# A hand-ordered opening of attention and MoE, put in another order on all five engines

## The chip, the core and the metric

The kernel runs on one core of a Trainium2 chip. The metric is the device time of one execution in microseconds (us). The kernel before was timed three times: 304.38, 303.49 and 304.17, median 304.17.

## What is computed

The reference chains two parts. Sliding-window causal attention over 8 batches of 8 heads with 576 tokens and 64 channels, in which a query sees itself and the 63 keys ahead of it, gives 4608 tokens of 512 channels; a feed-forward layer with the gate `h * cos(h)` follows.

```python
scores = scale * np.matmul(q, k.transpose(0, 1, 3, 2))
mask = (rel >= 0) & (rel < window)           # rel = query - key, window 64
scores = np.where(mask, scores, -1000000000.0)
attn = np.exp(scores - np.max(scores, axis=-1, keepdims=True))
attn = attn / (np.sum(attn, axis=-1, keepdims=True) + 1e-09)
x = np.matmul(attn, v)                       # then tokens x (heads * channels)
h = x @ w_in                                 # 512 -> 2048
g = h * np.cos(h)
out = g @ w_out                              # 2048 -> 512
```

## The kernel before

The feed-forward part goes over nine tiles of 512 tokens. In eight of them it runs in a steady state: TensorE (PE) is fed with `h` products (L468) and `out` products (L707 or L555) while the attention of the next batch is laid between them by planned times (`at`, `pump`). The first 58 us are different. There the first tile has nothing to hide behind, and every step is put out by hand: the string `FIRST` (L46) lists 303 tokens, and the loop at L671 carries them out one after the other. Each token issues a few instructions on one or two engines. So the place of a token in the string is the place of its instructions in the queue of their engine; the five engines take their queues strictly in order and meet only at semaphores. A last letter gives the engine: d is VectorE (DVE), a is ScalarE (ACT), p is GpSimd (POOL), s is a DMA from SyncE's queue (SP).

Work is cut by pairs of heads, p = 0 to 3, and a batch has 9 blocks of 64 queries. A group is four blocks of one pair; batch 0 has groups (p, 0) and (p, 1) for each pair. The tokens that matter, with their lines:

- `Lq0.p`, `Lk0.p`: q and k of one pair of batch 0 (`load_heads`, L155, a DMA from POOL's queue that casts to bf16; pair 0 comes as float32 by SP, `load_plain`, L162, and is cast by `cq` and `ck`). `Lq1`, `Lk1` are those of batch 1, `Lv0.c` a 128-token chunk of v, `Lwi.i` and `Lwo.i` quarters of w_in and w_out (L197, L200). `Lq2.c` and `Lk2.c` are 96-token chunks of batch 2 (L172).
- `io`, `mk`, `mc`: the distances by POOL (L137), the masks by DVE (L141 to L145), their bf16 copies by ACT (L149).
- `tq.p`, `tk.p`: 18 transposes of q or k on PE (L210); `pq`, `pk` copy them out of PSUM (L232, L234, L125). `Tq`, `Tk`, `Pq`, `Pk` are the same for batch 1.
- `s.p.g`: mask and scores of a group on PE (L314, L321); `m` its row maxima on DVE (L331); `e` four exponentials on ACT (L348); `i` the reciprocal of the sums on DVE (L358); `n` the normalising product, 128x512, on POOL or DVE (L365); `w` four transposes on PE (L381); `c` their copy (L389, carried out at L125).
- `zA`, `zB`, `zC`: each 64-token block of v must stand on both halves of the partitions; `spread_v` (L186) copies half a chunk to its neighbour, on DVE, POOL or by DMA on SP (L193).
- `v.a.g`: the values of two pairs on PE (L418); `x.a.g` copies them to `xT` (L425). `h.g.f` needs `x.0.g` and `x.1.g`: eight products with w_in (L432), half a token tile for two blocks of 128 features; `S.g.f` is the sine on ACT (L438), `g.g.f` the gate on DVE (L444). `o.q.m` is a quarter of an output tile on PE (L451).
- `Gs`, `Gm`, `Ge`, `Gi`, `Gn`, `Gw`, `Gc`, `Gp`: the same steps as s, m, e, i, n, w, c for the groups 8 to 18 (the rest of batch 0, and batch 1). Their maxima go by one instruction per block (L336).
- `f`: one 128x512 product that nobody reads (`keep_busy`, L129); eight of them run before the list.

Buffers join the queues. Transposes and values share three PSUM tiles (`ps_t`, L97), scores and `h` share five banks (L117, the last number of `s`, `Gs` and `h`), and a new user waits until the former one is read out. A DMA that POOL issues waits, as the eighth after another, for the landing of that one (its semaphore lane). After the list, `turn_k` (L248, planned at L610) transposes k of batch 2 by DMA on SP, chunk after chunk in the order 0 to 5, for the first scores of batch 2 (L299).

Of the kernel before, what the change touches and what calls it, by code (L numbers as in the profile page):

```python
# [10 lines left out]
def _safe_warn(msg, *a, **kw):  # L11
# [32 lines left out]


FIRST = (  # L46
# [19 lines left out]
)  # L66


# [1 line left out]
def kernel(  # L70
# [10 lines left out]
    B, H, S, D = q.shape  # L81
# [70 lines left out]
    def rows_tile(name):  # L152
        return ld.tile([128, NC * H * D], BF16, tag=name, name=name)

    def load_heads(name, b, p0=0, n=PAIRS):  # L155
        if (name, b) not in st:
            st[name, b] = rows_tile(name)[:, 0:PAIRS * RC * D].rearrange("p (a x) -> p a x", a=PAIRS)
        src = {"q": q, "k": k}[name][b, 2 * p0:2 * p0 + 2 * n]
        nc.gpsimd.dma_start(out=st[name, b][:, p0:p0 + n],
                            in_=src.rearrange("(a h) (p c) d -> (h p) a (c d)", h=2, c=RC))  # L160

    def load_plain(name):  # L162
        rows = moe.tile([128, 2, d_model], F32, tag="out", name="rows", bufs=OUTS).rearrange("p a f -> p (a f)")[:, 0:RC * D]
        st["rows", name] = rows
        nc.sync.dma_start(out=rows, in_={"q": q, "k": k}[name][0, 0:2].rearrange("h (p c) d -> (h p) (c d)", c=RC))
# [99 lines left out]
    for b in range(2, B):  # L265
        alone = NU // 2 if b == 3 else NU - 1
        steps = [(0, 2), (2, 4)], [(alone,)] + [(5, 7), (7, 9)] if b == 3 else [(4, 6), (6, 8), (alone,)]
# [362 lines left out]
    for n in range(16):  # L630
        i, f = divmod(n, 4)
# [14 lines left out]
    def spread_first(lo, hi):  # L646
        return lambda i, engine: spread_v(0, i, engine, lo, hi)

    steps = {"f": keep_busy, "Lq0": lambda p: load_heads("q", 0, p, 1) if p else load_plain("q"),
             "Lk0": lambda p: load_heads("k", 0, p, 1) if p else load_plain("k"),  # L650
             "cq": lambda engine: cast_plain("q", engine), "ck": lambda engine: cast_plain("k", engine),
             "Lq1": lambda p: load_heads("q", 1, p, 1), "Lk1": lambda p: load_heads("k", 1, p, 1),
# [24 lines left out]
    for mt in range(1, n_mt):  # L677
# [5 lines left out]
        for ff in range(n_ff):  # L683
# [8 lines left out]
            e = ff % 2  # L692
# [54 lines left out]
```

## Time and profile before

| what | value |
|---|---|
| median of three runs | 304.17 us (303.49 to 304.38) |
| the profiled execution | 303.55 us |
| its span, first to last instruction | 301.8 us |
| PE busy | 291.2 us, 97% of the span |
| DVE, ACT, POOL busy | 234.7, 232.3, 209.2 us |
| granted PE clock, mean | 0.993 |
| first `h` product (L432) starts | 22.18 us |
| first `h` product of the second token tile (L468) starts | 57.45 us |

The profiled execution is 1.75 us longer than its span (what lies before the first and after the last instruction) and 0.62 us shorter than the median. PE is busy almost all the time from 14 us on, so the table is read by stages of the opening: when the `h` products can start, and where PE waits between there and 57 us. A row of the timeline has the start and length in us, the engine, the line, the operation, what is written from what, its count, and in brackets the idle time just before and what ended it.

### The profile page before, as it was taken

To read this page: it belongs to the slowest core of one execution; us is meant where nothing else is said; L and a number is where in the kernel's file an instruction comes from. 1 tells how busy PE (TensorE), PEld (TensorE's weight loads), DVE (VectorE), ACT (ScalarE), POOL (GpSimd) and SP (SyncE) were. 2 spreads that over 40 slices of the span, in tenths; PEclk is the share of its full clock that TensorE was granted. 3 is DMA by queue.
4 is the path that set the end of the run, shared out by engine and by line. 5 is a ranking of instruction groups with operands and counts; after the bars stand their busy time and mean duration, and the time that the engine had idled before them with its cause. 6 is when DMAs were issued, how large, how long until landed. Compare 5 with 4: busy or idle time off the path is not lost.

```text
span 301.8 us, 8513 instructions
## 1 busy us (share of the span) xinstructions
PE 291.2 (97%) x2916; PEld 164.0 (54%) x2947; DVE 234.7 (78%) x916; ACT 232.3 (77%) x781; POOL 209.2 (69%) x238
## 2 busy tenths in 40 slices
PE   8799999999999999999999999999999999999996
PEld 3677854644455445444454445444544454785485
DVE  4798788888887886788668875887588658985794
ACT  5988699877987699869986999699978997304610
POOL 8979568986999589987998799878995860000000
PEclk9989999999999999999999999999999999999999
DMA  7999999999999994999999997999599935003013
GB/s 148 180 208 164 198 193 142 104 127 147 232 160 102 229 139 87 102 143 235 149 102 139 209 177 96 144 209 165 103 108 134 203 65 168 0 3 141 1 37 104
DMA packets 158732, 41.47 MB, mean 137 GB/s; under 512 B 146976, under 2 KB 154336, under 8 KB 158688
## 3 DMA queue, kind: packets, MB, share of 16 engines
q0 software_dynamic: 100192, 18.06, 79.8%
q1 hardware_dynamic: 58352, 22.79, 41.9%
q8 instruction: 23, 0.38, 0.5%
q14 instruction: 21, 0.17, 0.2%
q10 hardware_dynamic: 144, 0.07, 0.1%
HBM read 36.70 MB, written 9.44 MB: 153 GB/s over the span
## 4 chain that ended last, share of the span: by engine, by line
PE 88%; DMA 4%; DVE 3%; issue 2%; ACT 1%; POOL 1%; POOLq 0%; DVEq 0%
PE h_ps L468 37%; PE out_ps L707 27%; PE out_ps L555 8%; PE out_ps L451 4%; PE h_ps L432 3%; PE s_ps L299 3%; PE o_ps L400 3%; DMA w_in<-in_moe_w_in_dram 2%; DMA k<-in_k_dram 2%; PE tq_ps L213 1%; PE s_ps L321 1%; ACT e L348 1%; PE tk_ps L210 1%; DVE s L336 1%; PE tw_ps L381 1%
## 5 line engine op out<-in xcount | busy, mean ns | idle before, releaser
L468 PE MATMUL h_ps<-xT,w_in 128*128 128x512 bf16 x497 | 114.3, 379 | 1.0
L696 DVE TENSOR_TENSOR gT<-h_ps,sin 128x512 bf16<-128x512 f32 x128 | 85.2, 688 | 25.8 <-ACT sin L693 25.2
L693 ACT ACTIVATE sin<-h_ps 128x512 f32<-128x512 f32 x128 | 73.8, 598 | 37.1 <-PE h_ps L468 35.2
L348 ACT ACTIVATE e<-s,negm 128x128 f32<-128x128 f32 (+1 forms) x256 | 97.1, 382 | 1.7 <-POOL v L125 1.0
L707 PE MATMUL out_ps<-w_out,gT 128*128 128x512 bf16 x372 | 82.9, 379 | 1.7 <-issue 1.6
L365 POOL TENSOR_TENSOR w<-e,rden 128x512 bf16<-128x512 f32 (+1 forms) x68 | 69.1, 1032 | 18.0 <-DVE rden L358 15.1
L468 PEld LDWEIGHTS <-w_in 128*128 128x128 bf16 x512 | 49.0, 98 | 54.5
L707 PEld LDWEIGHTS <-gT 128*128 128x128 bf16 x384 | 36.5, 98 | 43.1
L336 DVE CUSTOM_DVE_ANT_0 s<-s_ps,mask 128x128 f32<-128x128 f32 (+1 forms) x256 | 56.0, 277 | 1.7 <-PE s_ps L321 1.4
L348 ACT ACTIVATION_READ_ACCUMULATOR e<-s,negm 128x1 f32 x256 | 48.1, 188 | 0.0
L176 POOL DMA_DIRECT2D q<-in_q_dram x36 | 28.6, 796 | 10.7 <-DMA q<-in_q_dram 5.4
L182 POOL DMA_DIRECT2D v<-in_v_dram x40 | 34.2, 870 | 1.2 <-DMA q<-in_q_dram 1.1
L176 POOL DMA_DIRECT2D k<-in_k_dram x36 | 28.6, 795 | 2.7 <-DMA v<-in_v_dram 1.9
L358 DVE RECIPROCAL rden<-den 128x4 f32<-128x4 f32 (+1 forms) x73 | 12.2, 167 | 18.3 <-ACT e L348 17.9
L125 POOL COPY v<-v 64x1536 bf16<-64x1536 bf16 (+3 forms) x16 | 22.9, 1433 | 0.4
L336 DVE DVE_READ_ACCUMULATOR2_ANT negm<- 128x1 f32 x256 | 21.2, 83 | 0.0
L125 DVE CAST xT<-o_ps 128x512 bf16<-128x512 f32 x24 | 15.5, 679 | 4.7 <-PE o_ps L400 4.5
L432 PE MATMUL h_ps<-xT,w_in 128*128 128x256 bf16 x128 | 14.8, 273 | 0.4 <-DMA w_in<-in_moe_w_in_dram 0.4
L451 PE MATMUL out_ps<-w_out,gT 128*128 128x512 bf16 x60 | 14.3, 380 | 0.3 <-issue 0.2
L432 PEld LDWEIGHTS <-w_in 128*128 128x128 bf16 x128 | 12.2, 98 | 2.1 <-DMA w_in<-in_moe_w_in_dram 0.7
L555 PEld LDWEIGHTS <-sums 128*128 128x128 bf16 x136 | 12.2, 98 | 1.9 <-DVE sums L500 0.4
L348 ACT ACTIVATE e<-s_ps,negm 128x128 f32<-128x128 f32 x32 | 11.3, 383 | 1.2 <-DVE negm L331 1.0
(88 smaller groups left out, 309.7 us busy)
## 6 DMA issues: line engine op xcount, KB each, us to landing
out_dram<-out_sb SPq DMA_DIRECT2D x16, 512.0 KB, 7.7
v<-in_v_dram POOLq DMA_DIRECT2D x32, 128.0 KB, 5.9
q<-in_q_dram POOLq DMA_DIRECT2D x36, 96.0 KB, 8.5
k<-in_k_dram POOLq DMA_DIRECT2D x36, 96.0 KB, 8.8
w_in<-in_moe_w_in_dram POOLq DMA_DIRECT2D x4, 512.0 KB, 8.8
w_out<-in_moe_w_out_dram POOLq DMA_DIRECT2D x4, 512.0 KB, 11.4
q<-in_q_dram POOLq DMA_DIRECT2D x7, 144.0 KB, 6.1
k<-in_k_dram POOLq DMA_DIRECT2D x7, 144.0 KB, 5.8
```

The source lines that it names most:

```text
L125: {"a": nc.scalar.copy, "p": nc.gpsimd.tensor_copy}.get(engine, nc.vector.tensor_copy)(out, in_)
L176: nc.gpsimd.dma_start(out=st[name, b][:, c].rearrange("p (h d) -> p h d", h=H), in_=src.rearrange("h p d -> p h d"))
L182: nc.gpsimd.dma_start(out=vt.rearrange("p (h d) -> p h d", h=H), in_=v[b, :, c * 128:c * 128 + n, :].rearrange("h p d -> p h d"))
L336: nc.vector.tensor_tensor_reduce(out=s[:, u, c], in0=s_ps[:, u, c], in1=mask[:, 2 - j % 2 if j else 0, c], scale=-scale if b else -1.0, sc ...
L348: nc.scalar.activation(e[:, u, c], s[:, u, c], AF.Exp, bias=negm[:, u:u + 1], scale=1.0 if n < n_first else -1.0, accum_out=den[:, u:u + 1])
L365: (nc.gpsimd if engine == "p" else nc.vector).tensor_tensor(out=w[:, 0:u], in0=e[:, 0:u], op=ALU.mult, in1=rden[:, 0:u].unsqueeze(2).to_br ...
L432: nc.tensor.matmul(out=h_ps[:, half * e:half * e + half], lhsT=w_in_sb[:, ks, ff * 128:ff * 128 + 128], rhs=st["xT", 0][:, ks, half * g:ha ...
L468: nc.tensor.matmul(out=st["h", ff], lhsT=w_in_sb[:, ks, ff * 128:ff * 128 + 128], rhs=st["xT", mt][:, ks], start=start, stop=stop)
L555: nc.tensor.matmul(out=to[n_] if split else to[:, e], lhsT=lhs[name][f // 2][:, f % 2, 128 * e:128 * e + 128], rhs=rhs[name][:, f, lo:hi], ...
L693: nc.scalar.activation(sin, h_ps, AF.Sin, bias=math.pi / 2.0)
L696: nc.vector.tensor_tensor(out=gt[:, e], in0=h_ps, in1=sin, op=ALU.mult)
L707: nc.tensor.matmul(out=o_ps[e], lhsT=gT[ff // 2][:, ff % 2, ms * 128:ms * 128 + 128], rhs=w_out_sb[:, ff], start=ff == 0, stop=ff == n_ff - 1)
```

## The change

`FIRST` is replaced by a list with the same steps in another order. Some steps change their engine or their bank as well. The dictionary of steps gets six names for `keep_busy` in place of one. Nothing else differs.

```diff
-    "io Lq0.0 Lk0.0 mk cq.d mc ck.a tq.0 f.1 Lq0.1 pq.0.d Lk0.1 tk.0 f.1 pk.0.a s.0.0.0 Lq0.2 tq.1 f.1 tk.1 m.0.0 "
+    "Lk0.0 Lq0.0 Lq0.1 Lk0.1 io mk Lq0.2 cq.d tq.0 ck.d Lk0.2 Lq0.3 mc tk.0 pk.0.a pq.0.d s.0.0.0 tq.1 s.0.1.3 "
...
-    steps = {"f": keep_busy, "Lq0": lambda p: load_heads("q", 0, p, 1) if p else load_plain("q"),
+    steps = {"fa": keep_busy, "fb": keep_busy, "fc": keep_busy, "fd": keep_busy, "fe": keep_busy, "ff": keep_busy, "Lq0": lambda p: load_heads("q", 0, p, 1) if p else load_plain("q"),
```

What moves, token by token, where the prediction speaks of it:

- `io` stands behind two of POOL's loads instead of ahead of all; `ck` goes from ACT to DVE.
- `Lk0.3` stands behind `Lq1.0` and `Lq1.1`. `pk.2` goes from DVE to ACT and stands behind `e.0.1`; `s.3.0` stands ahead of `Tk.0`, and `Tk.1` behind `s.3.1`.
- `Lwi.0` stands ahead of `Lv0.0`, `Lwi.1` ahead of `Lv0.2`; `n.0.0`, `n.2.0` and `n.1.0` stand between these loads, `n.3.0` behind `Lwi.2`. `Lwi.3` stands ahead of `n.0.1` and `n.2.1`; `n.1.1` and `n.3.1` go to DVE.
- `zA.0` goes from DVE to POOL, `zB.0` and `zC` from SP's DMA to DVE, `zB.1` from SP's DMA to POOL.
- two of the three `f` move from the first 7 us to just before `Tk.1` and just before `v.0.0`; `w.0.1` and `w.2.1` stand behind the first `h`.
- `Lk2.5` stands far ahead, `Lk2.3` ahead of batch 1's normalisations, and `Lk2.0` and `Lk2.1` are the last loads of the list.

POOL's queue from the last k of the first loads to the last quarter of w_in. v0 is batch 0's v; a row `w<-e,rden` is one normalisation. Before:

```order
L159 DMA k_326<-in_k_dram 128x576
L182 DMA v0_77<-in_v_dram 128x8x64 x4
L198 DMA w_in_79<-in_moe_w_in_dram 128x4x512 x3
L365 TENSOR_TENSOR w_499<-e_398,rden_462 128x512
L365 TENSOR_TENSOR w_531<-e_297,rden_396 128x512
L365 TENSOR_TENSOR w_534<-e_453,rden_469 128x512
L365 TENSOR_TENSOR w_570<-e_473,rden_536 128x512
L365 TENSOR_TENSOR w_587<-e_389,rden_572 128x512
L365 TENSOR_TENSOR w_678<-e_538,rden_589 128x512
L365 TENSOR_TENSOR w_720<-e_579,rden_656 128x512
L198 DMA w_in_79<-in_moe_w_in_dram 128x4x512
```

And the same stretch of the change, in which w_492 is `n.2.0`, w_515 `n.1.0` and w_582 `n.3.0`:

```order
L198 DMA w_in_79<-in_moe_w_in_dram 128x4x512
L182 DMA v0_77<-in_v_dram 128x8x64 x3
L198 DMA w_in_79<-in_moe_w_in_dram 128x4x512
L365 TENSOR_TENSOR w_435<-e_230,rden_259 128x512
L182 DMA v0_77<-in_v_dram 128x8x64
L365 TENSOR_TENSOR w_492<-e_461,rden_481 128x512
L365 TENSOR_TENSOR w_515<-e_428,rden_484 128x512
L198 DMA w_in_79<-in_moe_w_in_dram 128x4x512
L365 TENSOR_TENSOR w_582<-e_486,rden_538 128x512
L125 COPY v0_77<-v0_77 64x512
L159 DMA q_261<-in_q_dram 128x576
L198 DMA w_in_79<-in_moe_w_in_dram 128x4x512
```

The quarters of w_in have moved between v and the normalisations, and a copy of v stands behind `n.3.0`.

DVE's queue ahead of the copy to xT that the first `h` needs; the rows `kT` and `qT` are Pk and Pq, `negm` maxima, `wT` the copies c. Before, from `Pq.1`:

```order
L125 COPY qT1_76<-tq_ps_434 128x576
L331 TENSOR_REDUCE negm_520<-s_ps_501 128x4
L358 RECIPROCAL rden_536<-den_474 128x4
L125 COPY v0_77<-v0_77 64x512
L125 COPY wT_555<-tw_ps_544 128x512
L358 RECIPROCAL rden_572<-den_390 128x4
L125 COPY wT_574<-tw_ps_550 128x512
L125 COPY v0_77<-v0_77 64x512
L125 COPY wT_577<-tw_ps_565 128x512
L358 RECIPROCAL rden_589<-den_539 128x4
L125 COPY wT_617<-tw_ps_591 128x512
```

And of the change, from `i.3.0` to `x.0.0`; "..." stands for the other two blocks of `Gm.10`:

```order
L358 RECIPROCAL rden_538<-den_487 128x4
L125 COPY kT_479<-tk_ps_496 128x576
L358 RECIPROCAL rden_541<-den_285 128x4
L331 TENSOR_REDUCE negm_558<-s_ps_522 128x4
L125 COPY v0_77<-v0_77 64x512
L358 RECIPROCAL rden_584<-den_568 128x4
L336 ISA s_606,negm_605<-s_ps_560,mask_82 128x128
...
L125 COPY wT_610<-tw_ps_553 128x512
L125 COPY wT_614<-tw_ps_587 128x512
L365 TENSOR_TENSOR w_618<-e_567,rden_584 128x512
L125 CAST xT_637<-o_ps_620 128x2x256
```

`x.0.0` has come to DVE from ACT and stands behind `Gm.10` and a normalisation (w_618, `n.1.1`), while two of the copies c have gone to ACT.

The end of POOL's list, where the loads of batch 2 stand (q and k of 96x8x64), as a difference:

```order
 L125 COPY v_78<-v_78 64x2x512
-L365 TENSOR_TENSOR w<-e,rden 128x512
-L125 COPY v_78<-v_78 64x512
-L365 TENSOR_TENSOR w<-e,rden 128x512
-L176 DMA q<-in_q_dram 96x8x64 x3
-L176 DMA k<-in_k_dram 96x8x64 x6
+L176 DMA q<-in_q_dram 96x8x64 x4
+L176 DMA k<-in_k_dram 96x8x64
 L182 DMA v_78<-in_v_dram 64x8x64
+L176 DMA k<-in_k_dram 96x8x64 x3
 L182 DMA v_77<-in_v_dram 128x8x64 x4
```

Chunks 0 and 1 of k are now the last two of the three loads behind v, where they were the first two of six.

36 rows, old and new, of the table FIRST are left out of this document.

## The prediction

> **What bounds the kernel now.** The page first.
>
> ```profile
> span 301.8 us, 8513 instructions
> PE 291.2 (97%) x2916; PEld 164.0 (54%) x2947; DVE 234.7 (78%) x916; ACT 232.3 (77%) x781; POOL 209.2 (69%) x238
> ```
>
> PE is busy for 291.2 of 301.8 us. A new order removes no work, so it can only move the 10.6 us in which PE stands still, or the time at which it runs slowly. The stages of the opening show where (columns: stretch, its length, busy time of PE, PEld, DVE, ACT, POOL with counts, granted clock, DMA share, GB/s).
>
> ```profile
> 14.00:22.18 8.18, 7.60 (x160) 6.20 (x154) 7.20 (x25) 7.08 (x32) 6.55 (x8) 0.79 1.52 200
> 22.18:30.28 8.10, 7.68 (x99) 6.33 (x97) 6.95 (x30) 7.34 (x19) 7.35 (x10) 1.00 1.06 169
> 38.32:57.62 19.30, 18.89 (x260) 10.57 (x265) 16.34 (x81) 17.74 (x79) 15.51 (x19) 1.00 1.66 146
> ```
>
> From 22.18 us, when the first `h` starts, PE is full but for 0.42 us in the first stage and 0.41 in the last. So the end of the opening is the start of the first `h`, plus PE's work behind it, plus waits. PE's own timeline names these:
>
> ```profile
> 13.61 0.47 PE L210 MATMUL tk_ps<-ident,k 64*64 64x64 bf16 x18 [1.61 <-ACT e L348]
> 20.79 0.44 PE L418 MATMUL o_ps<-wT,v 128*64 128x64 bf16 x16
> 22.18 1.91 PE L432 MATMUL h_ps<-xT,w_in 128*128 128x256 bf16 x16
> 25.49 0.40 PE L381 MATMUL tw_ps<-ident,w 128*128 128x128 bf16 x4
> 30.28 8.03 PE L432 MATMUL h_ps<-xT,w_in 128*128 128x256 bf16 x72 [0.42 <-DMA w_in<-in_moe_w_in_dram]
> ```
>
> The chain that ended last names w_in between the two `h` rows:
>
> ```profile
> 23.10 7.13 DMA w_in<-in_moe_w_in_dram
> ```
>
> These 7.13 us are the age of the transfer, not a loss: PE ran seven `h` meanwhile and waited 0.42 us. The first `h` did not wait for w_in at all (its first quarter landed at 12.11 + 7.7 = 19.8 by the rows below); it waited for `x.1.0`, that is for `v.1.0` at 20.79 and the copy behind it. **So w_in ahead of v can gain 0.42 us and no more; what decides is when both halves of xT are there.**
>
> **The first `h` in the new order.** First POOL, DVE and ACT up to `e.3.0`, from their timelines:
>
> ```profile
> 1.27 0.53 POOL L137 IOTA mask<- 64x128 f32 x2
> 1.75 0.74 POOL L159 DMA_DIRECT2D q<-in_q_dram  x1
> 2.49 0.55 POOL L159 DMA_DIRECT2D k<-in_k_dram  x1
> 1.84 0.29 DVE L141 TENSOR_TENSOR mask<-mask 128x128 f32<-128x128 f32 x1 [0.69 <-POOL mask L137]
> 3.69 0.46 DVE L125 CAST q<-rows 128x576 bf16<-128x576 f32 x1 [0.60 <-DMA rows<-in_q_dram]
> 7.62 0.36 ACT L348 ACTIVATE e<-s_ps,negm 128x128 f32<-128x128 f32 x1
> 9.57 0.37 ACT L348 ACTIVATE e<-s_ps,negm 128x128 f32<-128x128 f32 x1 [0.45 <-DVE negm L331]
> 10.96 0.66 ACT L232 ACTIVATE qT<-tq_ps 128x576 bf16<-128x576 bf16 x1
> 15.51 0.37 ACT L348 ACTIVATE e<-s_ps,negm 128x128 f32<-128x128 f32 x1 [0.57 <-DVE negm L331]
> 16.08 0.73 DVE L125 COPY qT<-tq_ps 128x576 bf16<-128x576 bf16 x1
> 16.72 0.68 DVE L331 TENSOR_REDUCE negm<-s_ps 128x4 f32<-128x512 f32 x1
> ```
>
> `io` now waits for two issues (0.74 + 0.55), so the masks end at 4.33 instead of 3.08 and the cast of q behind them starts 0.6 later than at 3.69. That is partly won back: q and k have been on the chip since about 4 us, and ACT loses the cast of k. Adding the durations along the new order, with 0.04 from engine to engine: `e.0.0` at 7.7 (7.62 before), `e.0.1` at 9.95 (9.57). Then comes a wait that is new: `pk.2` stands behind `e.0.1` (four exponentials, 10.96 - 9.57 = 1.39) and ends at 12.0, and `s.2.0`, with the transposes queued behind it on PE (`tk.3`, `Tq.0`), waits for it from 10.85 on. That takes the place of the 1.61 ahead of 13.61. After it, 0.6 to 0.75 each: `m.2.0` to 13.15, `pk.3`, `Pq.0`, `m.3.0` to 15.2, and `e.3.0` at 15.2 to 16.6, where it was 15.51 to 16.9 (15.51 + 1.39). **So this part comes out 0.3 earlier, of no use by itself**, since DVE and POOL then hold it back (timelines; DMA issues with KB and us to landing; a line's durations in ns as min/median/max; a group's busy us and mean ns):
>
> ```profile
> 14.44 5.16 POOL L365 TENSOR_TENSOR w<-e,rden 128x512 bf16<-128x512 f32 x5
> 12.11 2.27 POOL L198 DMA_DIRECT2D w_in<-in_moe_w_in_dram  x3
> 8.62 3.53 POOL L182 DMA_DIRECT2D v<-in_v_dram  x4 [0.17 <-issue]
> w_in<-in_moe_w_in_dram POOLq DMA_DIRECT2D x1, 512.0 KB, 7.7
> w_in<-in_moe_w_in_dram POOLq DMA_DIRECT2D x1, 512.0 KB, 9.9
> 17.40 0.26 DVE L125 COPY v<-v 64x512 bf16<-64x512 bf16 x1
> 18.61 1.14 DVE L125 COPY v<-v 64x512 bf16<-64x512 bf16 x1
> 20.64 0.28 DVE L336 CUSTOM_DVE_ANT_0 s<-s_ps,mask 128x128 f32<-128x128 f32 x1
> 20.85 0.28 DVE L336 CUSTOM_DVE_ANT_0 s<-s_ps,mask 128x128 f32<-128x128 f32 x1
> 20.33 0.39 DVE L125 COPY wT<-tw_ps 128x512 bf16<-128x512 bf16 x1
> L365 DVE TENSOR_TENSOR w<-e,rden x5: 681/692/1458, 52.6 to 84.6; 128x512 bf16<-128x512 f32 x4, 128x384 bf16<-128x384 f32 x1
> L125 DVE CAST xT<-o_ps 128x512 bf16<-128x512 f32 x24 | 15.5, 679 | 4.7 <-PE o_ps L400 4.5
> ```
>
> POOL: the second quarter of w_in is issued at 11.55, when its lane is free, `n.0.0` ends at 13.35, a v at 14.2; `n.2.0` waits for `i.2.0` (15.35) and ends at 16.45, `n.1.0` at 17.45, the third quarter (0.76) at 18.2, `n.3.0` at 19.25. Before, `n.3.0` was the fourth of the five in the first row: 14.44 + 4 x 1.03 = 18.56. **0.7 later: the price of a normalisation behind a load issue.** `zA.0`, now on POOL, ends at 20.3.
>
> DVE: `m.3.0` ends at 15.2, then `i.2.0`, `Pq.1`, `i.1.0`, `m.3.1`, `m.1.1`, `i.3.0`, `Pk.1`, `i.0.1`, `m.2.1` (five at 0.6 to 0.7, four at 0.1) reach 18.7 to 19.3. Next is `zA.1`, and its price has two ends. The two v copies above have the same shape and took 0.26 and 1.14. POOL's normalisations ended at 17.53 and 19.60, and the copies 0.13 and 0.15 after that: each waited for the POOL instruction in flight. So `zA.1` ends at 19.4 if it is there before `n.3.0` ends at 19.25, and at 20.3 to 20.4 if `zA.0` has already started. Behind it stand `i.1.1` (0.1), `Gm.10` (3 x 0.21), `c.1.0` and `c.3.0` (0.4 each), `n.1.1` (0.69, the median of its row; the 1.46 there is the same shape) and `x.0.0` (0.68): 2.85. xT is complete at 22.25 or at 23.1; `x.1.0` on ACT is earlier (22.0). The filler product ahead of `v.0.0` waits for `Gm.10` as well, since they share a bank, so PE cannot run past this. Against 22.18 that is +0.07 or +0.92. The two estimates of DVE's arrival lie on both sides of 19.25; **I take the middle, +0.5.**
>
> The Trainium skill, "SBUF — State Buffer", section "Who interferes with whom", states this as a lock: a DVE copy in a fast mode, and a DVE product of two SBUF operands while GpSimd reads, blocks fully against a GpSimd instruction, and who starts first holds the port. The two copies agree; it speaks against this change, which adds `zB.0`, `zC`, `n.1.1` and `n.3.1` to DVE's side. By the lock alone, with every one of them losing, the sum would be rival A's; with none losing, this term would be +0.07.
>
> **From the first to the eighth `h`.** Before, 22.18 to 30.28: 8.10 us, in which 56 products (seven `h`, 8.03 / 9 = 0.89 each), `v.0.1`, `v.1.1` and four sets of transposes ran, and 0.42 was waiting. In the new order the wait goes: w_in's last quarter is issued at 20.9, not 23.10. Quarters land 2.9 apart (12.86 + 9.9 less 19.8), three of them with all of v by 25.6 before; one more and a q make 29.3, and the new list needs the last one only for the tenth `h`. `w.0.1` moves behind the first `h` (+0.2). New are waits of PE for normalisations that start later: `n.2.1` hangs on `i.2.1`, which stands on DVE behind `Gm.9`, `zC` and `Gm.12`, so it ends at 25.05 to 25.55 where PE arrives at 25.15 (0 to 0.5); `n.3.1`, on DVE behind `Gm.11`, `c.1.1` and `zB.0`, ends at 26.2 to 27.4 (0 to 0.7); `zB.1` on POOL behind two loads ends at 27.4 to 27.95, `v.0.1` behind it. PE starts the eighth `h` 7.75 to 8.7 after the first: -0.35 to +0.6, middle **+0.1**. `zB` and `zC` were DMAs, and none of PE's waits above names them, so taking them off the DMA saves nothing here, and two engines that are waited for get the work.
>
> **Behind that**, nine `h` at 0.89 and the 19.3 us of the last stage are the same work. S and g follow each `h` within the five banks; the score groups that come later now (`Gs.16`) are ready some 0.4 ahead of ACT's exponentials. **0.** The last term is batch 2's k (timelines of POOL, SP and PE, ages at landing, a group of the page):
>
> ```profile
> 55.24 4.58 POOL L176 DMA_DIRECT2D k<-in_k_dram  x6
> DMA to landing us min/median/max: 3.5/3.7/5.5
> L348 ACT ACTIVATE e<-s,negm 128x128 f32<-128x128 f32 (+1 forms) x256 | 97.1, 382 | 1.7 <-POOL v L125 1.0
> 59.06 8.66 SPq L249 DMA_TRANSPOSE kT<-k  x6
> kT<-k SPq DMA_TRANSPOSE x1, 7.5
> 72.40 0.59 PE L299 MATMUL s_ps<-kT,qT 64*64 64x64 bf16 x32
> ```
>
> The second and fifth rows are the age at landing of the six loads and of one transpose issued at 61.7. Chunk 0, issued at 55.24, let SP start at 59.06. Now it is next to last on POOL. `n.16` follows 28 blocks of exponentials (0.385 each) behind the table load that ends near 40.4: 51.2, with `n.16` and `yA` 53.3, and seven issues of 0.76 later 58.6; it lands at 62.3, and SP starts 3.3 later than before. The transpose that the first scores wait for, the third, landed at 61.7 + 7.5 = 69.2 and now lands at 72.5, just when PE comes to them (72.40, where the 32 products start). From 0 to 1.8 (a load that takes 5.5 and not 3.7); by the median, **0**.
>
> **The sum.** +0.5 + 0.1 + 0 + 0 = +0.6 on the profiled execution, whose 303.55 are the span and 1.75 around it that stay: 304.15. That execution is 0.62 below the median of 304.17, so in terms of the median the forecast is 304.8, within 0.3% (0.9 us), about what a measurement of this kernel can tell from no change.
>
> **The rivals.** *A, slower: DVE loses every meeting with POOL.* Then +0.92 and +0.6: +1.5, 305.7. It decides at `zA.1`: does it start before 19.25? For it: POOL's list between 18.2 and 28 has no idle time here, and PE ran at a lower clock in 14 to 22 us (0.79), which delays `m.3.1`. Against: a copy may meet a load issue instead of a normalisation, and no row shows that it waits for one. Chance 0.28. *C, slower: k of batch 2 late.* +0.6 and a wait of 1.2: 306.0; it decides from a landing of chunk 0 past 62.5. For it: no margin. Against: the 5.5 came with SP's transposes in flight, which here start later. Chance 0.12. *B, faster: DVE is not what holds xT.* If its list runs dense and the clock stays up, `n.3.0` at 19.25 decides: transposes 0.40, copy 0.39, values 0.44, x 0.68 give 21.2, -1.0; with the low end of the next term -1.35, 302.8. Against: eleven DVE instructions must then be done a microsecond earlier than their durations allow. Chance 0.18. *That the change does not do what it says*, w_in early without use, is in the forecast. It has 0.42.
>
> The Trainium skill, "TensorE: Matmul & The Clock Gate", section "What's actually happening", has the clock set by activity in windows of some 3.4 us that do not start with the kernel. The 0.79 agrees with one such stretch; where it falls in the new order no trace here shows. Were it gone, B would be likelier, by 0.3 us at `m.3.1`.
>
> The range: 303.1 leaves out the better part of B, 306.5 the worst of A and C together, some 0.17 in all. Faster by over 0.3% is B, 0.18; slower A and C, 0.40; within, 0.42.
>
> **What would show it.** Right: the first `h` at 22.2 to 23.1 with DVE's x just ahead; no PE wait for w_in; `n.3.0` ending past 19; small PE waits ahead of `w.2.1` or `w.3.1`. Wrong: a first `h` before 21.8 (B); v copies of 1 us and a first `h` past 23.1 (A); a PE wait ahead of L299 near 72 (C); or a wait of over 1 us between 30 and 57 us, which I hold for filled.

## The result, and the profile after

The changed kernel takes 306.53 us (median of four runs, 305.82 to 306.69), the kernel before 303.83 beside it (303.44 to 304.38): ratio 1.0083, 95% interval 1.0058 to 1.0108. It is slower by 2.7 us, by the medians. Here and below a ratio is taken against the kernel before, timed beside the version on the same chip, without the runs of a slower state that both kernels show now and then. The profiled execution after has 306.69 us and a span of 304.9. Its page begins:

```profile
span 304.9 us, 8521 instructions
PE 294.8 (97%) x2947; PEld 162.7 (53%) x2947; DVE 238.9 (78%) x921; ACT 231.5 (76%) x781; POOL 207.5 (68%) x236
```

PE's share is still 97%, so the page does not show where the time went. Busy time by stretches does, cut at PE's milestones: the first `h`, the end of the `h` products of the first token tile, the first `h` of the second tile, the end. Columns as in the prediction: stretch, length, busy time of PE, PEld, DVE, ACT, POOL, granted clock, DMA share, GB/s. After:

```profile
14.00:24.39 10.39, 8.14 (x199) 5.50 (x194) 10.13 (x25) 7.76 (x37) 8.64 (x11) 1.00 1.63 188
24.39:40.29 15.90, 15.78 (x176) 13.58 (x177) 13.67 (x45) 11.43 (x25) 9.12 (x12) 1.00 1.15 152
40.29:59.90 19.61, 19.24 (x265) 10.26 (x264) 17.23 (x83) 17.92 (x83) 15.33 (x18) 1.00 1.52 138
59.90:304.90 245.00, 241.41 (x2121) 127.51 (x2119) 190.26 (x753) 185.19 (x605) 162.56 (x173) 1.00 1.19 129
```

The last three of them in the kernel before:

```profile
22.18:38.32 16.14, 15.72 (x175) 13.38 (x174) 13.01 (x40) 12.33 (x27) 12.16 (x16) 1.00 1.21 183
38.32:57.45 19.13, 18.72 (x259) 10.47 (x264) 16.17 (x79) 17.57 (x79) 15.34 (x18) 1.00 1.65 147
57.45:301.80 244.35, 238.64 (x2094) 127.45 (x2119) 189.68 (x757) 185.07 (x607) 162.94 (x174) 1.00 1.19 130
```

So +2.21 us arise before the first `h` (24.39 for 22.18), -0.24 in the `h` run (15.90 for 16.14), +0.48 up to the second tile and +0.65 behind it: +3.10 in this execution. In the stretch before the first `h`, DVE is busy for 10.13 of 10.39 us, which points to DVE's list (a copy that is held up counts as busy). PE's timeline after, the rows with waits that count and the first `h`:

```profile
13.69 0.47 PE L210 MATMUL tk_ps<-ident,k 64*64 64x64 bf16 x18 [1.22 <-DMA k<-in_k_dram]
22.33 0.39 PE L132 MATMUL busy<-w_out 128*128 128x512 bf16 x1 [1.28 <-DVE negm L336]
24.39 1.91 PE L432 MATMUL h_ps<-xT,w_in 128*128 128x256 bf16 x16 [0.20 <-DVE xT L125]
56.36 0.40 PE L381 MATMUL tw_ps<-ident,w 128*128 128x128 bf16 x4 [0.37 <-DVE w L365]
```

No row waits for w_in any more. Two waits stand ahead of the first `h` that are new in this size: `tk.3` waits 1.22 for pair 3's k (0.18 before), and the filler waits for `Gm.10`, behind which x.0.0 is late as well. DVE's and POOL's timelines show why `Gm.10` is late, and the last two rows where the 0.37 comes from:

```profile
18.93 0.66 DVE L331 TENSOR_REDUCE negm<-s_ps 128x4 f32<-128x512 f32 x1
19.63 1.82 DVE L125 COPY v<-v 64x512 bf16<-64x512 bf16 x1
22.85 0.88 DVE L365 TENSOR_TENSOR w<-e,rden 128x512 bf16<-128x512 f32 x1
23.66 0.68 DVE L125 CAST xT<-o_ps 128x512 bf16<-128x512 f32 x1
19.22 1.05 POOL L365 TENSOR_TENSOR w<-e,rden 128x512 bf16<-128x512 f32 x1
20.20 0.61 POOL L125 COPY v<-v 64x512 bf16<-64x512 bf16 x1
20.76 0.61 POOL L159 DMA_DIRECT2D q<-in_q_dram  x1
22.12 1.06 POOL L365 TENSOR_TENSOR w<-e,rden 128x512 bf16<-128x512 f32 x1
54.73 1.03 POOL L125 COPY v<-v 64x1024 bf16<-64x1024 bf16 x1
55.20 1.11 DVE L365 TENSOR_TENSOR w<-e,rden 128x512 bf16<-128x512 f32 x1
```

`zA.1`, the copy at 19.63, takes 1.82 us; in the kernel before it took 1.14, and `zA.0`, of the same shape, 0.26. It starts inside POOL's `n.3.0`, and ends at 21.45, after `n.3.0` (20.27), `zA.0` (20.81) and POOL's load issue (21.37). From its end to the first `h` are 2.94 us of dense DVE work.

### The profile page after: what moved, and what is told of

Same layout as the page of the kernel before. It is cut to its first block, busy times and chain, and to the rows that moved or that the text cites. A ratio compares the mean times of both kernels' runs of the same rounds, so it can differ in the third digit from the quotient of the medians.

```text
span 304.9 us, 8521 instructions
## 1 busy us (share of the span) xinstructions
PE 294.8 (97%) x2947; PEld 162.7 (53%) x2947; DVE 238.9 (78%) x921; ACT 231.5 (76%) x781; POOL 207.5 (68%) x236
## 4 chain that ended last, share of the span: by engine, by line
PE 79%; DMA 8%; POOL 5%; SPq 2%; DVE 2%; issue 2%; ACT 0%; POOLq 0%
PE h_ps L468 33%; PE out_ps L707 23%; PE out_ps L555 8%; DMA wT<-w 5%; PE out_ps L451 4%; PE h_ps L432 3%; PE o_ps L400 3%; DMA k<-in_k_dram 3%; PE s_ps L299 2%; SPq L249 2%; POOL w L365 2%; PE tq_ps L213 1%; POOL q L159 1%; PE s_ps L321 1%; POOL v L125 1%
## 5 line engine op out<-in xcount | busy, mean ns | idle before, releaser
L365 POOL TENSOR_TENSOR w<-e,rden 128x512 bf16<-128x512 f32 (+1 forms) x65 | 66.8, 1042 | 31.6 <-DVE rden L358 29.2
L707 PE MATMUL out_ps<-w_out,gT 128*128 128x512 bf16 x384 | 85.3, 379 | 0.0
L358 DVE RECIPROCAL rden<-den 128x4 f32<-128x4 f32 (+1 forms) x73 | 12.2, 167 | 19.6 <-ACT e L348 19.4
L125 POOL COPY v<-v 64x1024 bf16<-64x1024 bf16 (+3 forms) x17 | 23.5, 1383 | 0.5
L125 DVE CAST xT<-o_ps 128x512 bf16<-128x512 f32 x26 | 16.9, 677 | 4.3 <-PE o_ps L400 4.3
L451 PE MATMUL out_ps<-w_out,gT 128*128 128x512 bf16 x64 | 15.0, 380 | 0.0
L125 ACT CAST xT<-o_ps 128x512 bf16<-128x512 f32 x10 | 5.8, 583 | 9.3 <-PE o_ps L400 7.3
```

What stands on the lines that cost most here:

```text
L125: {"a": nc.scalar.copy, "p": nc.gpsimd.tensor_copy}.get(engine, nc.vector.tensor_copy)(out, in_)
L365: (nc.gpsimd if engine == "p" else nc.vector).tensor_tensor(out=w[:, 0:u], in0=e[:, 0:u], op=ALU.mult, in1=rden[:, 0:u].unsqueeze(2).to_br ...
L707: nc.tensor.matmul(out=o_ps[e], lhsT=gT[ff // 2][:, ff % 2, ms * 128:ms * 128 + 128], rhs=w_out_sb[:, ff], start=ff == 0, stop=ff == n_ff - 1)
```

## The experiments

Two theories stood at first. P: DVE's copy of v meets POOL and waits. L: a load is late, pair 3's k, since it is issued as the eighth of POOL's loads and not as the sixth. A third, W, has the same k late because w_in's first quarter is now issued soon behind it. Four kernels, each an edit of the changed list.

**Pair 3's k early.**

```diff
-Lq1.0 pq.2.a tk.2 Lq1.1 e.0.1 pk.2.a tq.3 s.1.0.4 Lk0.3 s.1.1.1
+Lk0.3 Lq1.0 pq.2.a tk.2 Lq1.1 e.0.1 pk.2.a tq.3 s.1.0.4 s.1.1.1
```

> The changed list with one token moved: pair 3's k (Lk0.3) is issued ahead of batch 1's first two q, as in the kernel before. Theory L (a load is late): the first h came 2.2 late because the transposes tk.3 waited 1.22 us for this k, which landed at 13.64; with two issues less ahead of it it lands near 11.5, the wait goes, e.3.0 and n.3.0 come 1.0 to 1.2 earlier, and so does the first h (24.39 to 23.2 to 23.4): -1.0 to -1.2 us against the change. Theory P (the port): the first h is held by DVE's v copy of 1.82 us, which waited out three POOL instructions; those come earlier, but the copy meets them as before, since DVE gets there earlier too: the copy still takes over 1 us, and the time moves by -0.3 to -0.8. Theory W (w_in's first quarter fills the DMA engines ahead of k): the k still lands only with the others, near 12.5, -0.5.

The first `h` came at 23.42, as L has it, and `tk.3` did not wait. But the copy on DVE still took 1.77 us, and the ratio is 1.0073 (1.0029 to 1.0117): no gain in time. PE's timeline shows where it went:

```profile
23.42 3.32 PE L432 MATMUL h_ps<-xT,w_in 128*128 128x256 bf16 x16
```

The same 16 products took 1.91 in the change. The clock granted from 22.9 to 26.3 us was a half in this execution.

**`zA.1` on ACT.**

```diff
-zA.1.d c.2.0.a
+zA.1.a c.2.0.a
```

> The changed list with one copy of v (zA.1) carried out by ACT in place of DVE; nothing else moves. Theory P (the port): the 1.82 us on DVE go, the maxima Gm.10, c.1.0, c.3.0, n.1.1 and x.0.0 behind it come up to 1.5 us earlier, and the first h starts at 22.8 to 23.2: -1.2 to -1.6 us. Theory L (pair 3's k is late): n.3.0 still ends at 20.27, and the transposes, copy, values and x behind it need 1.9 to 2.4 more with a normalisation on DVE between, so the first h stays at 23.6 or later: -0.8 at most. On ACT the copy should take its own time, about 0.5 us, whatever POOL does.

Ratio 1.0028 (0.998 to 1.0075). Timelines of ACT, DVE, POOL and PE:

```profile
18.68 0.62 ACT L125 COPY v<-v 64x512 bf16<-64x512 bf16 x1
22.33 0.71 DVE L125 COPY v<-v 64x512 bf16<-64x512 bf16 x1
22.00 0.95 POOL L182 DMA_DIRECT2D v<-in_v_dram  x1
22.04 1.91 PE L432 MATMUL h_ps<-xT,w_in 128*128 128x256 bf16 x16
57.50 2.75 PE L468 MATMUL h_ps<-xT,w_in 128*128 128x512 bf16 x12
```

On ACT the copy takes 0.62 with `n.3.0` in flight. The first `h` is at 22.04 and that of the second tile at 57.50: the kernel before had 22.18 and 57.45. That is more than P forecast, because pair 3's k was in time in this execution as well; with k in time, the copy accounts for all that the opening still lost. The ratio alone does not settle it: its interval holds 1 and overlaps the change's own. The second row is a new meeting: `zC` on DVE took 0.71, starting inside a load issue of POOL and ending 0.09 behind it.

**Both edits.** (The two diffs together.)

> Both edits: pair 3's k early, and zA.1 on ACT. If the two causes are in series (the late k delays n.3.0, and the copy then waits for n.3.0), the two together give about -2.2 us, which brings the first h to 22.2 and the time to that of the kernel before, 303.8. If one of them is the whole cause, this is no better than that one alone: -1.2 to -1.5. Past the opening the waits of 0.37 at 56.36 and of 0.31 at 185.4 may stay: then 0.5 us above the kernel before.

Ratio 1.0017 (0.9972 to 1.0061), first `h` at 22.13. It is no better than `zA.1` on ACT alone, because pair 3's k was not late there.

**v ahead of w_in again.**

```diff
-Lk1.0 Lwi.0 Lv0.0 Lv0.1 Lv0.3 pq.3.d
+Lk1.0 Lv0.0 Lv0.1 Lv0.3 Lv0.2 Lwi.0 pq.3.d
...
-s.3.1.3 Lv0.2 Pk.0.a
+s.3.1.3 Pk.0.a
```

> The changed list with the first quarter of w_in put back behind the four loads of v, where the kernel before has it, so that no w_in is issued before 11 us. Theory W: the k of pair 3 landed at 13.64, 2.2 us behind the load before it, because w_in's 512 KB were issued at 8.85 and shared the engines; without it the k lands near 12.3, the wait of 1.22 ahead of tk.3 shrinks below 0.3, and the time falls by 0.8 to 1.2 us. Theories L and P: the gap in the landings has nothing to do with w_in, the first h stays at 24.2 to 24.5, and so does the time, within 0.4 us; w_in's fourth quarter lands as before. As the prediction had it, w_in early is without use, so nothing is lost either.

Ratio 1.0102 (1.0001 to 1.0203): nothing won back. The first `h` came at 23.71, with `zA.1` at 1.73 us and 2.93 from its end to `h`. The k landed at 12.09, so W is possible by this run alone; the landings below show that w_in ahead of v is not enough to make it late.

The second four ask what the copy waits for, and try single parts in the kernel before.

**`zA.0` on ACT, `zA.1` on DVE.**

```diff
-zA.0.p
+zA.0.a
```

> The changed list with the other copy of v (zA.0) carried out by ACT in place of POOL; zA.1 stays on DVE. POOL then issues two loads (0.61 and 0.75 us) right behind n.3.0. Theory P1 (only POOL's computing instructions hold the copy on DVE): zA.1 ends 0.15 behind n.3.0 and takes some 1.0 us or less in place of 1.82; the first h comes 0.8 to 1.0 earlier. Theory P2 (POOL's load issues hold it too): zA.1 ends 0.1 behind the end of the first or the second issue, 0.7 to 1.5 behind n.3.0, and takes 1.2 to 2.0 us; the first h comes at most 0.6 earlier. If zA.1 gets in ahead of n.3.0, it takes 0.3, the theories are not told apart by it, and the first h comes over 1.5 earlier.

Ratio 1.006 (1.0021 to 1.0099). DVE and POOL:

```profile
19.94 1.27 DVE L125 COPY v<-v 64x512 bf16<-64x512 bf16 x1
19.53 1.05 POOL L365 TENSOR_TENSOR w<-e,rden 128x512 bf16<-128x512 f32 x1
20.51 0.60 POOL L159 DMA_DIRECT2D q<-in_q_dram  x1
```

The copy ended at 21.21: 0.63 behind `n.3.0` and 0.10 behind the load issue. So P2, the issue holds it as well, and `zA.0` on POOL was only a part of it. The first `h` (24.14) is 2.93 behind that end. On this chip the two versions with `zA.1` on ACT stand at 1.0028 and 1.0017, and the three with a ratio that leave it on DVE at 1.006, 1.0073 and 1.0102: the times lean the way the traces do.

**Without the filler.**

```diff
-c.1.0.d fa.1 c.3.0.d
+c.1.0.d c.3.0.d
```

> The changed list without the filler product ahead of v.0.0 (a product that nobody reads), on which PE waited 1.28 us for Gm.10. Theory P (DVE's list holds x.0.0): the first h comes within 0.2 us of where it was, 24.2 to 24.5; the wait of 1.28 turns into waits ahead of the values or of h. Rival F (the filler's wait, in a bank it shares with Gm.10, held PE): the values start where PE stands free, at 21.1, and the first h comes 1.0 or more earlier.

306.58 us in one run, with 304.08 for the kernel before beside it. The wait of 1.28 split into 0.59 and 0.60 ahead of the values. The first `h` was at 23.35, but not because of the filler: DVE reached `zA.1` 1.04 earlier (18.59), and from the copy's end to `h` were 2.94 again. F falls.

**Before, with `zA.0` on POOL.**

```diff
-n.0.0.p Pk.1.a n.2.0.p i.3.0 e.1.1 w.0.0 zA.0.d w.1.0 c.0.0.d Gs.12.0 w.2.0 n.3.0.p
+n.0.0.p Pk.1.a n.2.0.p i.3.0 e.1.1 w.0.0 w.1.0 c.0.0.d Gs.12.0 w.2.0 n.3.0.p zA.0.p
```

> The list of before with one edit: zA.0 on POOL, right behind n.3.0, and no longer on DVE. Theory P: zA.1 on DVE, which took 1.14 at 18.61 behind n.3.0, now waits out zA.0 as well (0.61): it takes 1.6 to 1.8, c.2.0 and what is behind it comes 0.5 later, and the first h, which hangs on the copies c and v behind zA, comes 0.3 to 0.6 later (22.5 to 22.8); DVE's 0.26 saved on zA.0 gives little back. Rival (the place of a copy on DVE matters, not POOL): DVE has one copy less, the first h comes 0.1 to 0.3 earlier.

Ratio 0.9998 (0.9967 to 1.0028), first `h` at 21.93. P's expectation failed. DVE and POOL:

```profile
18.37 0.81 DVE L125 COPY v<-v 64x512 bf16<-64x512 bf16 x1
18.97 0.67 POOL L125 COPY v<-v 64x512 bf16<-64x512 bf16 x1
```

Here the copy got in when `n.3.0` ended (19.02) and `zA.0` was the one to be held up, 0.67 for 0.61. A copy of POOL behind the normalisation does not always win.

**Before, with w_in's first quarter ahead of v.**

```diff
-s.2.0.4 Lv0.0 Lv0.1 Tq.0 Lv0.2
+s.2.0.4 Lwi.0 Lv0.0 Lv0.1 Tq.0 Lv0.2
...
-Lv0.3 Lwi.0 Pq.0.d
+Lv0.3 Pq.0.d
```

> The list of before with one edit: the first quarter of w_in is issued ahead of the four loads of v, the change's best-known part by itself. As the prediction had it, w_in early is without use: the first h waits for x.1.0, not for w_in, and stays at 22.2; the wait of 0.42 at 30.28 is for the last quarter, which stays where it is, so the time stays within 0.3 us, or gets 0.3 to 0.6 worse if v, one issue of 0.76 later, then holds zA or v.0.0. Rival: the first h comes earlier by 0.3 or more, since w_in was late after all.

Ratio 1.0026 (0.9984 to 1.0068): no gain, and a loss is not settled by the times. In the trace the first `h` came 0.85 later, at 23.03, and DVE now waited for v ahead of `zA`:

```profile
18.06 0.85 DVE L125 COPY v<-v 64x512 bf16<-64x512 bf16 x1 [0.53 <-DMA v<-in_v_dram]
```

The last four: the copy once more, a version meant to beat both kernels, and the change itself again.

**The load issues later.**

```diff
-c.3.0.d Lq1.2 Lwi.3 n.1.1.d v.0.0 x.0.0.d v.1.0 n.0.1.p
+c.3.0.d n.1.1.d v.0.0 x.0.0.d v.1.0 n.0.1.p Lq1.2 Lwi.3
```

> The changed list with the two load issues that stood behind zA.0 on POOL (a q and the last quarter of w_in) put behind n.0.1, so that POOL runs n.3.0, zA.0, n.0.1 without an issue between; zA.1 stays on DVE. Theory P2 (the load issues hold the copy on DVE, and between two computing instructions of POOL it gets in): zA.1 ends 0.15 behind n.3.0 or behind zA.0, takes 0.9 to 1.5 us in place of 1.82, and the first h, 2.75 to 2.95 behind its end, comes 0.5 to 1.1 earlier. Theory P1 (only what POOL computes holds it): zA.1 waits out n.0.1 as well and ends 1.5 or more behind n.3.0's end; the first h comes later than in the change. The last quarter of w_in comes 1.0 later, which is still in time for the tenth h.

Ratio 1.0138 (1.0086 to 1.019), the worst of all, with the first `h` at 24.73. A part of that is the load: pair 3's k was late in this execution, and `tk.3` waited 1.44 us for it. DVE and POOL:

```profile
20.48 1.52 DVE L125 COPY v<-v 64x512 bf16<-64x512 bf16 x1
20.23 0.61 POOL L125 COPY v<-v 64x512 bf16<-64x512 bf16 x1
20.80 1.03 POOL L365 TENSOR_TENSOR w<-e,rden 128x512 bf16<-128x512 f32 x1
23.11 0.91 POOL L182 DMA_DIRECT2D v<-in_v_dram  x1
23.40 0.68 DVE L365 TENSOR_TENSOR w<-e,rden 128x512 bf16<-128x512 f32 x1
```

The copy started inside `zA.0`, waited out `n.0.1` too, and ended 0.17 behind it (22.00): P1 this time. Taking the issues away only put another instruction of POOL in their place. The last two rows show that the normalisation `n.1.1` on DVE is not held by a load issue (0.68).

**Before, with a load issue behind `n.3.0`.**

```diff
-n.3.0.p i.0.1
+n.3.0.p Lwi.3 i.0.1
...
-n.2.1.p c.0.1.d Lwi.3 w.2.1
+n.2.1.p c.0.1.d w.2.1
```

> The list of before with one edit: the last quarter of w_in is issued right behind n.3.0 (0.8 us) in place of behind n.2.1. Theory P2: the copy of v on DVE that waited for n.3.0 now also waits for this issue, ends 0.1 behind the issue's end and 0.7 to 0.9 later than before; the first h comes 0.5 to 0.9 later (22.7 to 23.1), and the wait of 0.42 for w_in goes: +0.1 to +0.5 us in all. Theory P1: the copy gets in at the end of n.3.0 as before, the first h stays at 22.2 or comes 0.3 later with n.0.1, and with the wait of 0.42 gone the time falls by 0.1 to 0.4.

Ratio 1.0017 (0.9985 to 1.0048), first `h` at 22.19. P2's expectation failed:

```profile
18.90 0.34 DVE L125 COPY v<-v 64x512 bf16<-64x512 bf16 x1
19.03 0.81 POOL L198 DMA_DIRECT2D w_in<-in_moe_w_in_dram  x1
```

The copy got in at the end of the normalisation (19.09) although a load issue followed. The wait for w_in is gone, as expected, but the times do not show a gain; in the profiled execution PE waited 1.82 us at 57.3 for a DMA that turns w, more than in any other trace (about 0.5 at most).

**The meetings taken away.**

```diff
-zA.1.d c.2.0.a e.2.1
+zA.1.a c.2.0.d e.2.1
...
-Gn.13.p Lq2.1 Ge.15 Gi.16 Gn.16.p
+Gn.13.p Lq2.1 Ge.15 Gi.16 yA.p Gn.16.p
...
-Gw.16 yA.p Gc.9
+Gw.16 Gc.9
```

> The changed list with DVE's meetings taken away: zA.1 on ACT, c.2.0 on DVE in its place, and the copy yA of POOL ahead of n.16 so that the DVE product n.15 no longer runs into it. By the theory that these meetings are the whole loss, the first h starts at 21.6 to 21.9 (22.04 with zA.1 on ACT alone), the wait of 0.37 ahead of Gw.15 goes, and the time is 0.3 to 0.8 us below the kernel before: 303.0 to 303.5 by the level of the first runs. If something else in the new order costs time as well, it stays at the level of the kernel before or above.

Ratio 1.0054 (1.0032 to 1.0077): a miss. In the profiled execution the first `h` came at 24.26: pair 3's k was late again (`tk.3` waited 1.32), and the moves made new meetings. DVE, POOL and PE:

```profile
22.05 1.56 DVE L365 TENSOR_TENSOR w<-e,rden 128x512 bf16<-128x512 f32 x1
21.99 1.06 POOL L365 TENSOR_TENSOR w<-e,rden 128x512 bf16<-128x512 f32 x1
53.31 1.32 DVE L365 TENSOR_TENSOR w<-e,rden 128x512 bf16<-128x512 f32 x1
56.55 0.69 DVE L365 TENSOR_TENSOR w<-e,rden 128x512 bf16<-128x512 f32 x1
54.69 0.40 PE L381 MATMUL tw_ps<-ident,w 128*128 128x128 bf16 x4 [0.95 <-DVE w L365]
57.30 0.40 PE L381 MATMUL tw_ps<-ident,w 128*128 128x128 bf16 x4 [0.32 <-DVE w L365]
```

`n.1.1` arrived 0.06 after POOL's `n.0.1` had started and waited it out, 1.56 for 0.68; with `zA.1` alone on ACT it had run at 20.24, ahead of `n.0.1`. At 53 us the moved copy `yA` (52.92 to 54.08) left `n.15` alone, which took 0.69, and held `n.8`, which stands ahead of it on DVE, for 1.32: a wait of 0.95 ahead of `Gw.8` is new, and that ahead of `Gw.15` is still 0.32. No version here beat the kernel before.

**The change again.** (No edit.)

> The changed kernel itself again, on the chip of the three others, for a second look at what differs between executions. Theory P2: the copy zA.1 again ends 0.1 behind the end of POOL's load issue that follows zA.0, and the first h again 2.9 us behind that. The landing of pair 3's k (13.64, 2.2 behind the load before it) is the open point: if it comes near 11.5 to 12.5 this time, the wait ahead of tk.3 is a matter of the execution and not of the order, the first h comes up to 1.0 earlier, and the time is 1.7 to 2.7 us above the kernel before.

Ratio 1.0067 (1.0042 to 1.0093). ACT, DVE, POOL and PE, then the stretch of the first two `h` by clock:

```profile
15.24 0.47 ACT L348 ACTIVATE e<-s_ps,negm 128x128 f32<-128x128 f32 x1
18.61 1.82 DVE L125 COPY v<-v 64x512 bf16<-64x512 bf16 x1
18.20 1.05 POOL L365 TENSOR_TENSOR w<-e,rden 128x512 bf16<-128x512 f32 x1
19.19 0.61 POOL L125 COPY v<-v 64x512 bf16<-64x512 bf16 x1
19.74 0.60 POOL L159 DMA_DIRECT2D q<-in_q_dram  x1
23.37 3.54 PE L432 MATMUL h_ps<-xT,w_in 128*128 128x256 bf16 x16 [0.20 <-DVE xT L125]
```

```profile
23.37:26.91 3.54, 3.54 (x19) 2.48 (x19) 3.50 (x28) 2.96 (x9) 1.58 (x2) 0.52 1.28 203
```

Pair 3's k was in time here, so everything up to `zA.1` runs 1.02 us ahead of the first execution; the copy again takes 1.82, ends 0.09 behind the load issue (20.43), and the first `h` follows 2.94 later. Then the half clock takes 1.63 back (3.54 for 1.91), of which 1.27 are left at the end of the `h` products (23.37 to 40.54, for 24.39 to 40.29).

The landings tell the load apart from the order. The ages at landing of the two loads issued as seventh and eighth, in the first execution of the change and in the second:

```profile
DMA to landing us min/median/max: 6.1/6.9/7.7
```

```profile
DMA to landing us min/median/max: 5.9/6.0/6.1
```

The eighth is pair 3's k: 5.92 + 7.7 = 13.6 in the one, 6.00 + 6.1 = 12.1 in the other, same kernel. So w_in's place alone does not make the load late: it was the same in both. Over the eight traces in which this k is the eighth load, its age at landing was 5.9 to 6.2 us five times (one of them with v ahead of w_in) and 7.6 to 7.7 three times (the first execution, the later issues, the meetings taken away). Whether w_in ahead makes the late landing possible is open, since a single trace has it elsewhere. As the sixth load, in the kernel before, the k was nearly in time:

```profile
10.57 0.47 PE L210 MATMUL tk_ps<-ident,k 64*64 64x64 bf16 x18 [0.18 <-DMA k<-in_k_dram]
```

## Why the prediction was right or wrong

The forecast, within 0.3%, did not come; what came is rival A, DVE losing its meetings with POOL. Its 305.7 was still too low because two things came on top that no term of the sum held: a late load in the first execution, a stretch of half clock in the second.

- **w_in: right.** The wait of 0.42 went and nothing more: -0.24 in the `h` run. In the kernel before, w_in ahead of v gains nothing and makes v later.
- **The opening up to `e.3.0`: right, with a term missing.** In the second execution `e.3.0` starts at 15.24 (predicted 15.2), and the new wait of `s.2.0` ends at 12.16 (12.0), though it is 0.69 and not 1.15, since PE got there later. But my sum named no landing for pair 3's k: it put at nothing a load that had moved from the sixth place to the eighth. There it landed at 12.1 or at 13.6; before, at 10.5, with a wait of 0.18. Where it is late, `e.3.0` comes 1.0 later: of the 2.21 in the first execution, 1.02.
- **POOL: right.** `n.3.0` ends at 19.25 in the second execution. That it agrees to the digit is luck (`n.0.0` ended 0.5 later than I had it, and the wait of `n.2.0` for `i.2.0` took that up); `zA.0` at 19.80, earlier than the 20.3 assumed.
- **DVE: the step that failed.** It said that `zA.1` ends at 19.4 "if it is there before `n.3.0` ends at 19.25". It was there at 18.61, 0.64 ahead of that, and ended at 20.43. The rule was read from two copies of the kernel before, which both got in 0.13 to 0.15 behind the instruction in flight. Behind the first of these another normalisation followed at once and did not win; behind the second POOL had nothing to do for 0.89 us. I had no row in which a following instruction won. The other end, 20.3 to 20.4, agrees with 20.43 by luck: it counted `zA.0` at some 1.05 us (it took 0.61) and no load issue, and the issue made up the rest. The 2.85 behind it was right (2.94). So both outcomes should have been at the late end: +1.19 in the second execution where I took +0.5. With `zA.1` on ACT, and k in time as well, the first `h` came at 22.04: that shows the cause of this part in the trace.
- **First to eighth `h`: the waits I feared did not come, the clock did.** PE waited for no normalisation there. In the first execution the eighth `h` starts 7.9 us after the first (the sixth at 30.51, and two of 0.89), for 8.10 before: -0.2 where I took +0.1. But in the second execution the half clock fell on these products, +1.63. Of the ten runs of the change in this second measurement, the five at a mean clock of 0.994 have a median of 306.52, the four at 1.000 one of 304.89 (one at 0.999 took 306.92). The clock is not the whole of it: three of the four runs of the first measurement had a clock of 1.000 and took 305.82 to 306.69, the profiled one with the late k. In the kernel before, the stretch lay at 14 to 17.5 us; there a lower mean clock goes with 0.4 us (303.98 for 303.59, medians of 9 and 18 runs beside the second measurement). That it moved because PE now stands idle longer ahead of the first `h` is argued, not shown.
- **Behind that: 0 was too low.** The 0.37 at 56.36 is the same mechanism: `n.15` on DVE took 1.11 for 0.69, starting inside POOL's `yA` and ending 0.55 behind it. Of the +0.65 behind 59.90, 0.31 is one wait at 185.4 for a DMA that turns w; the rest is not explained, and with the same list there the version with `zA.1` on ACT has 244.40 for 245.00.
- **kT of batch 2: right, with no margin.** Nothing waits for it in the first execution, whose PE is late; with v ahead of w_in and with `zA.0` on ACT, PE waited 0.5 and 0.4 for it; with `zA.1` on ACT, whose PE is on time, it did not wait.

The Trainium skill, "SBUF — State Buffer", section "Who interferes with whom", had the direction of all this: a DVE copy in its fast mode blocks against GpSimd. It also infers that a product of two SBUF operands does not conflict with descriptor generation, which `n.1.1` at 23.40 beside the issue at 23.11 (0.68) bears out; that a copy does, `zC` shows (0.71 inside an issue). The prediction cited the lock and gave rival A 0.28.

**Open:** which instruction gets the port at a boundary. With a normalisation in flight and more of POOL's queue behind it, the copy got in at its end in the kernel before (`zA.0`, 17.53) and in two edits of it (`zA.1`, 19.02 and 19.09), and waited on in every version of the changed list that left it on DVE. In six of those seven it ended 0.08 to 0.17 behind the end of a later instruction of POOL, a load issue five times; with pair 3's k early it ended inside the second load issue. No run tells what differs.

## What to carry to other kernels

Before work is moved between DVE and POOL, look for what runs on the other of the two at that moment; a short copy on DVE may cost not its 0.26 us but the rest of one, two or three POOL instructions, and ACT, idle or not, may be the better place (0.62 here). A wait that is taken away on one engine moves all later meetings, so price the list by ranges at the late end. And the landing of a load that the path hangs on needs a term of its own, with its spread: here it came 1.5 us later in one execution than in another.

## What the runs showed of the hardware that was not expected

- A DVE copy of 64x512 bf16 took 0.26 to 1.82 us, by what POOL did meanwhile; a normalisation of 128x512 took 0.68 to 1.56, and ended 0.55 behind POOL's instruction in flight.
- The stretch of half clock lasts some 3.4 us (a mean of 0.52 over 3.54 us is a half for 3.4 of them) and lies elsewhere, or nowhere, in another execution: between 14 and 19 us in the kernel before, two edits of it and two of the change, between 22.9 and 27.3 in the second execution of the change and two of its edits, and in none of the other six, the first execution of the change among them. One edit of the kernel before had a second stretch, from 58.4 to 61.8, behind its wait of 1.82 us. The Trainium skill, "TensorE: Matmul & The Clock Gate", section "What's actually happening", gives windows of some 3.4 us; the length agrees.
- The eighth load of POOL's queue landed 6.1 or 7.7 us after its issue in two executions of one program, and in none of eight traces between 6.2 and 7.6.
